# State stages on four whole PSUM banks shared by both diagonals, without filler stages

## The chip, the cores and the metric

The kernel runs on one core of one Trainium2 chip. Five engines have instruction queues of their own, each worked off in order: TensorE (PE in the profile, its weight loads PEld), VectorE (DVE), ScalarE (ACT), GpSimd (POOL) and SyncE (SP), which issues the DMAs here. Matmul results go to PSUM, whose 128 partitions have eight banks of 512 float32 each; DVE and ACT read them there. The metric is the device time of one execution in microseconds, lower is better, as the median of several runs.

## The reference

First a delta rule over 768 steps, for each of 4 batches and 8 heads, with a state of 48 x 48; then a gated MLP over the heads' joined outputs.

```python
for t in range(S):                       # S = 768, per batch and head
    kt, vt, bt = k_n[:, :, t], v[:, :, t], beta[:, :, t, None]
    y[:, :, t] = einsum('bhd,bhde->bhe', q[:, :, t], state)
    v_old = einsum('bhde,bhd->bhe', state, kt)
    state = state + bt[..., None] * einsum('bhd,bhe->bhde', kt, vt - v_old)
x = y.transpose(0, 2, 1, 3).reshape(B, S, H * D)
h = maximum(x @ w_in, 0);  u, v = halves of h
v_n = (v - mean(v)) / sqrt(var(v) + 1e-6)
v_s = einsum('ts,bsd->btd', w_spatial, v_n) + b_spatial[None, :, None]
out = (u * v_s) @ w_out
```

k_n is k divided by its norm. All inputs are float32, and the output has shape 4 x 768 x 384.

## The kernel before

The recurrence is worked in chunks of 64 steps: 12 chunks for each of 4 batches, 48 chunk steps s. Two chains run beside each other: batches 0 and 2 in one, 1 and 3 in the other, six chunks behind; ORDER interleaves them. A chunk step handles all 8 heads, as 4 units of two heads each; one head of a unit lies on partitions 0 to 63, the other on 64 to 127.

Each chunk step has stages on PE of 8 small matmuls (64 x 64 blocks, two heads by four units; step d has 16). A stage writes a tile `pt` in PSUM, and one instruction on DVE or ACT reads it, the stage's reader:

- kk (L574): k times k, ahead of time; reader DVE L595, which makes the matrix to be inverted in `ta`
- e and f (L705): complete the inverse T of that matrix; readers ACT L717 (`pi`) and ACT L729 (`ta`)
- a (L733): state times k; reader DVE L748 (`vk`)
- b (L753): T times that; reader DVE L764 (`us`)
- c (L773): update of the state; reader DVE L792 (`st`)
- qk (L796): q times k; reader DVE L808 (`aq`)
- d (L814): the chunk's output; reader ACT L837 (`xs`)

The chain through the state is a, b, c and again a of the same chain's next chunk. T comes from DVE: groups of four chunk steps are bounced through DRAM, inverted lane by lane with products and sums (`lanes`, L635 and L642) and bounced back.

A 64 x 64 stage uses half of PE's 128 x 128 array: its two heads lie either on the diagonal (kind "diag": e, f, c, qk) or on the other one (kind "anti": kk, a, b, d). One stage of each kind can run together, their matmuls issued in turn.

The MLP (L894 to L1069) has matmuls over the whole array ("full"): v and u from the finished outputs of four chunks, g with w_spatial when a whole batch is there, and o with w_out. They use the banks `pm` and, once the last lanes are done, `pw`.

The order in which each engine gets its instructions is not written by hand. A planner (class Line) runs when the program is built: every job is a generator that yields its next Op with an engine, an estimated occupancy and latency, a function that says when its inputs are ready, and a due time. Line.step takes the engine that can begin first and, among the operations ready within a small slack, the one with the earliest due time. For PE, Line.tensor chooses between full operations and stages. It takes a full operation when the activity of the last 3.4 us (area) is low and one is ready; otherwise an urgent operation, a pair of kinds, a full one, or a single stage. keep_warm inserts matmuls on `ones` (L1239) when PE would be idle and activity is low. Once a stage is picked, L179 looks for one of the other kind that is ready within 0.2 us. If there is none and the area is below FILL, a filler (L1248) takes its place: as many matmuls on `mpos`, into a free tile of the other kind, whose result nobody reads.

The result of every stage goes to a slot of a Slots object: take gives the slot that came free first, and the job gives it back when the planner has placed the reader. Before, four banks `pt0` to `pt3` are cut into eight halves of 256 columns. Each kind has four slots, two halves each of two banks:

```python
banks = [ps.tile([128, 512], F32, name=f"pt{i}") for i in range(4)]
halves = [x[:, o : o + 256] for x in banks for o in (0, 256)]
...
slots = {"anti": Slots(halves[:4]), "diag": Slots(halves[4:])}
```

tiles_op (L414) makes a stage's Op: it is ready when its inputs are and a slot of its kind is free. The planner knows slots only by these free times. The waits on semaphores that the chip executes are derived by the framework from the tiles that the instructions touch.

Of the kernel before, what the change touches and what calls it, by code (L numbers as in the profile page):

```python
# [72 lines left out]
class Line:  # L73
# [4 lines left out]
    def __init__(self, t0):  # L78
        self.t = dict.fromkeys(("PE", "DVE", "ACT", "POOL", "SP"), t0)
        self.done = {}  # L80
        self.jobs = []
        self.mode = "full"
        self.cur = 0
        self.hist = []
        self.idle = self.fake = None

    def at(self, *names):
        done = self.done
# [64 lines left out]
    def tensor(self, e0, near):  # L153
        tiles = [f for f in near if f[1].kind != "full"]
        full = [f for f in near if f[1].kind == "full"]

        def first(fs):
            return min(fs, key=lambda f: (f[1].due(), f[0]), default=None)

        kinds = {k: [f for f in tiles if f[1].kind == k] for k in ("anti", "diag")}  # L160
        low = self.area(e0) < LOW
        urgent = [f for f in near if f[1].due() <= self.cur + URGENT]
        pick = first(full) if low else first(urgent)
        if pick is None and all(kinds.values()):
            if self.mode == "tile" or not full or first(tiles)[1].due() <= self.cur + PAIR:
                pick = first(tiles)
        pick = pick or first(full) or first(tiles)
        t, op, j = pick
        self.keep_warm(t)
        t = max(t, self.t["PE"])  # L170
        change = 0.12 if (op.kind == "full") != (self.mode == "full") else 0.0
        slow = self.slow(t)
        if op.kind == "full":
            self.mode = "full"
            self.t["PE"] = t + change + op.occ * slow
            self.hist.append((self.t["PE"], op.occ * 2300))
            return self.grant(j, t + change + op.occ * slow + op.lat - op.occ)
        self.mode = "tile"
        f = first([f for f in kinds["anti" if op.kind == "diag" else "diag"] if f[0] <= t + 0.2])  # L179
        picked = [(op, j)]  # L180
        if f:
            picked.append(f[1:])
            t = max(t, f[0])
        lists = [o.make() for o, _ in picked]
        act_ = sum(o.lat * len(x) for (o, _), x in zip(picked, lists))
        if not f and self.area(t) < FILL:
            more = self.fake("anti" if op.kind == "diag" else "diag", t, len(lists[0]))
            if more:
                lists.append(more)
                act_ += 62 * len(more)  # L190
        for k in range(max(map(len, lists))):
            for x in lists:
                if k < len(x):
                    x[k]()
        end = t + change + 0.056 * slow * max(map(len, lists))
        self.t["PE"] = end
        self.hist.append((end, act_))
        for _, k in picked:
            self.grant(k, end + 0.22)
# [36 lines left out]
def delta_rule_gated_mlp(  # L236
# [107 lines left out]
    sss, nrs, t0s = ([sb(f"{n}{i}", G * NU) for i in range(2)] for n in ("ss", "nr", "t0"))  # L344

    banks = [ps.tile([128, 512], F32, name=f"pt{i}") for i in range(4)]
    halves = [x[:, o : o + 256] for x in banks for o in (0, 256)]
    pms = [ps.tile([128, 512], F32, name=f"pm{i}") for i in range(2)]
    pws = [ps.tile([128, 512], F32, name=f"pw{i}") for i in range(2)]

    class Slots:
        def __init__(self, tiles):
            self.free = [(0.0, k, x) for k, x in enumerate(tiles)]

        def ready(self):
            return min(self.free)[0] if self.free else None

        def take(self):
            f = min(self.free)
# [3 lines left out]
        def give(self, x, t):  # L363
            self.free.append((t, *x))

    slots = {"anti": Slots(halves[:4]), "diag": Slots(halves[4:])}
    ob_s = Slots([sb(f"ob{i}", DM) for i in range(1)])
    tmp_s, pm_s, xs_s, vh_s, ub_s = Slots(tmps), Slots(pms), Slots(xsb), Slots(list(zip(vhs, vls))), Slots(ubs)

# [27 lines left out]
    def rows_s(h):  # L397
        return rows_t(1 - h)
# [9 lines left out]
    def psl(t, w):  # L408
        return t[:, : NU * w].rearrange("p (u e) -> p u e", e=w)

    def mm(*a, **k):
        return lambda: nc.tensor.matmul(*a, **dict(dict(start=True, stop=True), **k))  # L412

    def tiles_op(kind, dep, d, build, w):  # L414

        held = []

        def make():
            x = slots[kind].take()
            held.append(x)  # L420
            return build(psl(x[1], w))

        return Op("PE", 0, 1.3 * w, both(dep, slots[kind].ready), d, kind, make), held


    def load_w(buf, hi, lo, src, d):
# [147 lines left out]
    def kk(t):  # L574
        g = t // G
        d = due(4 * g - 9)
        k = kts[t % 2] if t >= 2 * G else (
            xsb[t // 4][0:KR, t % 4 * 256 : t % 4 * 256 + 256].rearrange("p (u t) -> p u t", t=CH)
        )
        yield dma(at(("pk", t - 2) if t >= 2 * G + 2 else None), due(4 * g - 11), 3.5 if t < 2 * G else 6.0, 1.0)  # L580
        nc.sync.dma_start(out=k, in_=kq_t[t][:, 0])
        landed = line.t["SP"] + (3.0 if t < 2 * G else 5.5)
        free = [("b", s) for s in range((g - TG) * G, (g - TG) * G + G)] if g >= TG else []
        op, held = tiles_op(
            "anti",
            both(on(landed), at(("mc", t) if t >= G else None, *free)),
            d,
            lambda p: [mm(p[rows_t(h), u], k[rows_d(h), u, :], k[rows_d(h), u, :]) for u, h in UH],
            CH,
        )  # L590
        x = yield op
        done["pk", t] = x
        x = yield dve(both(on(x), at(("mc", t))), d, 256)
        p = held[0]
        nc.vector.tensor_tensor(out=t_of(t), in0=psl(p[1], CH), in1=mcs[t % 2], op=ALU.mult)  # L595
        slots["anti"].give(p, x)
        done["kk", t] = x

    ad_g = {}
# [105 lines left out]
    def step_ef(s):  # L705
        tt, tn, pi = t_of(s), tns[s % 2], pis[s % 2]
        op, held = tiles_op(
            "diag",
            at(("t", s), ("f", s - 2) if s >= 2 else None),
            due(s - 1),  # L710
            lambda p: [mm(p[rows_t(h), u], tt[rows_t(h), u, :], tn[rows_t(h), u, :]) for u, h in UH],
            32,
        )
        x = yield op
        done["e", s] = x
        x = yield act(on(x), due(s - 0.9), 128, 1)
        nc.scalar.mul(out=pi[:, :, 0:32], in_=psl(held[0][1], 32), mul=hl)  # L717
        slots["diag"].give(held[0], x)
        op, held = tiles_op(
            "diag",  # L720
            on(x),
            due(s - 0.8),
            lambda p: [mm(p[rows_t(h), u], pi[rows_t(h), u, :], tt[rows_t(h), u, 32:64]) for u, h in UH],
            32,
        )
        x = yield op
        done["f", s] = x
        x = yield act(on(x), due(s - 0.7), 128)
        nc.scalar.copy(out=tt[:, :, 32:64], in_=psl(held[0][1], 32))  # L729
        slots["diag"].give(held[0], x)  # L730
        done["fa", s] = x

    def step_ab(s):  # L733
# [3 lines left out]
        if c:  # L737
            op, held = tiles_op(
                "anti",
                at(("S", s), ("kq", s), ("vs", s)),  # L740
                due(s - 0.5),
                lambda p: [mm(p[rows_t(h), u], kq[rows_d(h), 0, u, :], cols(st, u, rows_d(h))) for u, h in UH],
                HD,
            )
            x = yield op
            done["a", s] = x
            x = yield dve(on(x), due(s - 0.45), 192)
            nc.vector.tensor_add(out=v, in0=v, in1=psl(held[0][1], HD))  # L748
            slots["anti"].give(held[0], x)
        else:  # L750
            done["a", s] = x = 0.0
        old = prev(s, 2)
# [14 lines left out]
            in1=css[s // G][:, s % G].unsqueeze(2).broadcast_to([128, NU, HD]),  # L767
            op=ALU.mult,
        )
        slots["anti"].give(held[0], x)  # L770
        done["U", s] = x

    def step_c(s):  # L773
# [16 lines left out]
        x = yield dve(on(x), due(s + 0.12), 192)  # L790
        lo = slice(0, KR)
        nc.vector.tensor_add(out=heads(nx, lo), in0=heads(st, lo), in1=psl(held[0][1], HD)[lo])  # L792
        slots["diag"].give(held[0], x)
        done["S", PLACE[b, c + 1]] = x

    def step_qk(s):  # L796
# [9 lines left out]
        done["qk", s] = x  # L806
        x = yield dve(on(x), due(s + 0.85), 256)
        nc.vector.tensor_tensor(out=aq, in0=psl(held[0][1], CH), in1=mall, op=ALU.mult)  # L808
        slots["diag"].give(held[0], x)
        done["q", s] = x  # L810

    xcur = {}
# [1 line left out]
    def step_d(s):  # L814
# [20 lines left out]
        xt = xcur[ch][1].rearrange("p (u t) -> p u t", t=256)  # L835
        x = yield act(on(x), due(s + 1.3), 256)
        nc.scalar.mul(out=xt[0:112, :, qt * 64 : qt * 64 + 64], in_=psl(held[0][1], CH)[0:112], mul=-1.0)  # L837
        slots["anti"].give(held[0], x)
        done["xs", s] = x
        if qt == 3:  # L840
            line.spawn(convert((b * NC_ + c) // 4, xcur[ch], x))
# [392 lines left out]


    def idle(t):
        free = [f[2][:, 0:256] for k in (pm_s, slots["anti"], slots["diag"]) for f in k.free if f[0] <= t]
        if free:
            nc.tensor.matmul(  # L1239
                free[0].rearrange("p (n t) -> p n t", t=128),  # L1240
# [4 lines left out]
            )  # L1245
        return bool(free)

    def fake(kind, t, n):  # L1248

        free = [f[2] for f in slots[kind].free if f[0] <= t]  # L1250
        if not free:
            return None
        p = psl(free[0], HD)
        r = [
            mm(p[rows_t(h) if kind == "diag" else rows_s(h), u], mpos[rows_t(h)], mpos[rows_t(h), 0:HD])
            for u, h in UH
        ]
        return (r * 2)[:n]

    line.idle, line.fake = idle, fake  # L1260
    ET = mybir.EngineType
    with tc.manual_schedule(engines={ET.PE, ET.DVE, ET.Activation, ET.Pool, ET.SP}):
        seen = {"s": 0, "g": 0}
# [74 lines left out]
```

## Time and profile before

| | |
|---|---|
| median of 3 runs | 595.15 us (591.41, 595.15, 597.2) |
| the profiled execution | 594.68 us, span of its instructions 593.0 us |
| mean granted TensorE clock in it | 0.902 |
| matmuls on ones (L1239) | 228 |
| filler matmuls (mpos, L412) | 288 |
| DMA moved | 64.31 MB, mean 108 GB/s |

The profile is of one execution. A group's row has the line of the kernel, the engine, the operation, output<-inputs by the program's names without their numbers, the shape and the count; then the busy time in us, the mean of one in ns, and the time that the engine was idle before such instructions, with what released it. A timeline's row has start and duration in us, engine, line, operation, and in brackets the idle time before it and the releaser. All stages are recorded at L412, the helper that issues their matmuls; the operands tell them apart.

The span has three parts. Up to some 60 us the first chunks' inverse is made and weights are loaded. From 60 to 400 us the chains and the lanes run with MLP work between them, and behind 400 us the MLP's work prevails, with the last stages in between until 530 us.

### The profile page before, as it was taken

The page shows a single profiled execution, that of the slowest core. Times are in us where ns is not written, and L with a number is a line of the kernel's source. Part 1 is how long each engine was busy: PE and PEld are TensorE (multiplying, and loading weights), DVE is VectorE, ACT ScalarE, POOL GpSimd, SP SyncE. Part 2 cuts the span into 40 slices and gives each one's busy share as a digit, 9 for nine tenths or more (in the row PEclk, how much of TensorE's full clock was granted, in tenths as well). Part 3 has the DMA queues.
Part 4 walks back from the last instruction along what each step waited for, and adds up shares of the span by engine and source line. Part 5 has one row for each costly group of instructions (what it writes and reads, how often), then busy time and mean ns, then how long its engine had stood idle before and what let it go on. Part 6 is the DMA issues. An engine that isn't in the chain of part 4 may idle for free.

```text
span 593.0 us, 22265 instructions
## 1 busy us (share of the span) xinstructions
PE 521.4 (88%) x9404; PEld 474.3 (80%) x9404; DVE 352.9 (60%) x1436; ACT 216.8 (37%) x536; POOL 139.5 (24%) x210
## 2 busy tenths in 40 slices
PE   5935889889778997979999989999999999988997
PEld 5834868778657786979997878889988899977996
DVE  5799585977857988857995685871135422132220
ACT  3224334532334556223326456321256511155111
POOL 5452233652235242312204153120000000000000
PEclk9675586978878999979999899999999999997999
DMA  8767385676935766457736536333012200010001
GB/s 222 213 109 168 92 175 146 182 193 135 222 99 132 178 138 134 103 148 143 179 67 118 154 86 141 120 92 77 28 32 72 67 14 15 28 33 2 1 28 55
DMA packets 140160, 64.31 MB, mean 108 GB/s; under 512 B 107542, under 2 KB 130204, under 8 KB 140060
## 3 DMA queue, kind: packets, MB, share of 16 engines
q1 hardware_dynamic: 140060, 62.88, 43.7%
q8 instruction: 74, 1.21, 0.9%
q14 instruction: 26, 0.21, 0.1%
HBM read 47.55 MB, written 14.02 MB: 104 GB/s over the span
## 4 chain that ended last, share of the span: by engine, by line
PE 58%; DVE 18%; DMA 8%; SPq 6%; issue 5%; ACT 4%; POOL 1%; DVEq 0%; ACTq 0%; POOLq 0%
PE pt L412 21%; PE pm L1001 9%; PE pm L969 6%; PE pw L1001 6%; DVE prod L635 4%; DVE pw L642 4%; PE pm L1056 4%; PE pm L903 3%; PE pw L1056 3%; PE pw L903 2%; DMA kq<-in_kq_t 2%; PE pw L969 1%; SPq L861 1%; DVE ta L595 1%; SPq L619 1%
## 5 line engine op out<-in xcount | busy, mean ns | idle before, releaser
L642 DVE TENSOR_TENSOR pw<-pw,prod 128x30 f32<-128x30 f32 (+6 forms) x330 | 81.6, 251 | 5.4
L635 DVE TENSOR_TENSOR prod<-pw,la 128x30 f32<-128x30 f32 (+6 forms) x330 | 78.7, 241 | 6.9 <-ACT pw L629 1.7
L412 PE MATMUL pt<-kq,st 48*64 48x64 f32 x768 | 56.3, 239 | 2.1 <-ACT xs L837 1.7
L1001 PE MATMUL pm<-wsp_h,vh 128*128 128x256 f32 x192 | 57.4, 299 | 0.0
L412 PE MATMUL pt<-aq,us 64*64 64x64 f32 x768 | 54.4, 235 | 3.3 <-issue 3.0
L1001 PE MATMUL pm<-wsp_l,vh 128*128 128x256 f32 x192 | 54.7, 285 | 0.0
L1001 PE MATMUL pm<-wsp_h,vl 128*128 128x256 f32 x192 | 54.6, 284 | 0.0
L688 POOL TENSOR_TENSOR vk<-vk,cn 128x192 f32<-128x192 f32 x48 | 24.5, 512 | 116.7 <-DMA vk<-in_vk_nat 97.9
L412 PEld LDWEIGHTS pt<-aq,us 64*64 64x64 f32 x768 | 45.0, 149 | 3.5 <-issue 3.1
L412 PEld LDWEIGHTS pt<-kq,st 48*64 48x64 f32 x768 | 44.8, 148 | 3.6 <-ACT xs L837 1.8
L569 POOL TENSOR_TENSOR mc<-mpos,cn 128x256 f32<-128x256 f32 x46 | 28.9, 638 | 62.1 <-DVE cn L557 27.9
L412 PE MATMUL pt<-kq 48*64 48x64 f32 x768 | 37.9, 241 | 5.3 <-DMA kq<-in_kq_t 3.9
L412 PE MATMUL pt<-tn,ta 64*64 64x32 f32 x768 | 35.3, 237 | 7.3 <-DVE tn L703 3.8
L1239 PE MATMUL pm<-ones 128*128 128x256 f32 x216 | 39.5, 333 | 2.5 <-ACT ones L274 2.5
L1037 ACT CAST gh<-tmp 128x512 fp32r<-128x512 f32 x24 | 14.8, 619 | 70.3 <-DVE tmp L1018 70.2
L412 PE MATMUL pt<-us,vk 64*64 64x48 f32 x704 | 33.6, 235 | 7.5 <-DVE us L764 6.6
L412 PEld LDWEIGHTS pt<-tn,ta 64*64 64x64 f32 x768 | 30.8, 154 | 10.9 <-DVE tn L703 5.7
L412 PE MATMUL pt<-ta,pi 64*64 64x32 f32 x768 | 35.5, 235 | 3.8 <-ACT pi L717 2.0
L412 PE MATMUL pt<-k 48*64 48x64 f32 x640 | 30.4, 242 | 9.2 <-DMA k<-in_kq_t 6.8
L1001 PEld LDWEIGHTS pm<-wsp_h,vh 128*128 128x128 f32 x192 | 36.9, 192 | 1.5
L1018 DVE TENSOR_TENSOR tmp<-pm,ub 128x512 f32<-128x512 f32 x16 | 11.0, 688 | 45.4 <-PE pm L1004 45.4
L412 PEld LDWEIGHTS pt<-us,vk 64*64 64x64 f32 x704 | 28.1, 147 | 12.0 <-DVE us L764 8.8
(182 smaller groups left out, 1500.4 us busy)
## 6 DMA issues: line engine op xcount, KB each, us to landing
kq<-in_kq_t SPq DMA_DIRECT2D x48, 224.0 KB, 3.5
vk<-in_vk_nat SPq DMA_DIRECT2D x48, 200.0 KB, 3.4
ad<-ta SPq DMA_DIRECT2D x24, 256.0 KB, 4.2
la<-ad SPq DMA_DIRECT2D x44, 128.0 KB, 4.0
out<-ob SPq DMA_DIRECT2D x24, 192.0 KB, 1.9
k<-in_kq_t SPq DMA_DIRECT2D x40, 112.0 KB, 3.5
knn<-in_k_nat SPq DMA_DIRECT2D x10, 384.0 KB, 4.4
wd<-w SPq DMA_DIRECT2D x22, 128.0 KB, 3.6
```

Source lines behind the costliest of these rows:

```text
L412: return lambda: nc.tensor.matmul(*a, **dict(dict(start=True, stop=True), **k))
L569: (nc.vector if t in (0, 2) else nc.gpsimd).tensor_tensor(out=mc, in0=mall, in1=cns[t // G][:, t % G, 1].unsqueeze(2).broadcast_to([128, N ...
L635: nc.vector.tensor_tensor(out=pr, in0=w[:, :n, j : j + 1].broadcast_to([128, n, m]), in1=la[:, j, j + 1 : 32].unsqueeze(1).broadcast_to([1 ...
L642: nc.vector.tensor_add(out=w[:, :n, j + 1 : 32], in0=w[:, :n, j + 1 : 32], in1=pr)
L688: nc.gpsimd.tensor_tensor(out=v, in0=v, in1=cns[s // G][:, s % G, 0].unsqueeze(2).broadcast_to([128, NU, HD]), op=ALU.mult)
L903: nc.tensor.matmul(p[1], a[:, kt, ts], w[:, kt, DH:], start=(n == 0), stop=(n == 3 * NK - 1))
L969: nc.tensor.matmul(pu[:, k], w[:, kt, d0 : d0 + 128], a[:, kt], start=(n == 0), stop=(n == 3 * NK - 1))
L1001: nc.tensor.matmul(pg[:, k], v[:, d0 : d0 + 128], w[:, si, ts], start=(n == 0), stop=False)
L1018: nc.vector.tensor_tensor(out=gt, in0=pg, in1=ut[:, hs], op=ALU.mult)
L1037: nc.scalar.copy(out=gh[:, hs], in_=gt)
L1056: nc.tensor.matmul(p[1][:, :DM], a[:, dd, ts], w[:, dd], start=(n == 0), stop=(n == 3 * ND - 1))
L1239: nc.tensor.matmul(free[0].rearrange("p (n t) -> p n t", t=128), ones, ones.unsqueeze(1).broadcast_to([128, 2, 128]), start=True, stop=True,)
```

## The change

The eight halves become four slots, the first 256 columns of each of the four banks, in one Slots object for both kinds. A stage of either kind takes whichever came free first. A second stage is only paired with the picked one if two slots are free by then (`room`, the time at which the second slot is free, at most 0.2 us after the first stage's time), and the pair starts no earlier than that. The fillers go. All `slots["anti"]` and `slots["diag"]` in the steps become `st_s`; the matmuls, readers, due times and costs stay.

```diff
-        f = first([f for f in kinds["anti" if op.kind == "diag" else "diag"] if f[0] <= t + 0.2])
+        room = self.room(2)
+        other = kinds["anti" if op.kind == "diag" else "diag"]
+        f = None
+        if room is not None and room <= t + 0.2:
+            f = first([f for f in other if f[0] <= t + 0.2])
         picked = [(op, j)]
         if f:
             picked.append(f[1:])
-            t = max(t, f[0])
+            t = max(t, f[0], room)
         lists = [o.make() for o, _ in picked]
         act_ = sum(o.lat * len(x) for (o, _), x in zip(picked, lists))
-        if not f and self.area(t) < FILL:
-            more = self.fake("anti" if op.kind == "diag" else "diag", t, len(lists[0]))
-            if more:
-                lists.append(more)
-                act_ += 62 * len(more)
...
     banks = [ps.tile([128, 512], F32, name=f"pt{i}") for i in range(4)]
-    halves = [x[:, o : o + 256] for x in banks for o in (0, 256)]
...
-        def ready(self):
-            return min(self.free)[0] if self.free else None
+        def ready(self, n=1):
+            return sorted(self.free)[n - 1][0] if len(self.free) >= n else None
...
-    slots = {"anti": Slots(halves[:4]), "diag": Slots(halves[4:])}
+    st_s = Slots([x[:, 0:256] for x in banks])
+    line.room = st_s.ready
...
         def make():
-            x = slots[kind].take()
+            x = st_s.take()
             held.append(x)
             return build(psl(x[1], w))
 
-        return Op("PE", 0, 1.3 * w, both(dep, slots[kind].ready), d, kind, make), held
+        return Op("PE", 0, 1.3 * w, both(dep, st_s.ready), d, kind, make), held
...
-        free = [f[2][:, 0:256] for k in (pm_s, slots["anti"], slots["diag"]) for f in k.free if f[0] <= t]
+        free = [f[2][:, 0:256] for k in (pm_s, st_s) for f in k.free if f[0] <= t]
...
-    def fake(kind, t, n):
-
-        free = [f[2] for f in slots[kind].free if f[0] <= t]
-        if not free:
-            return None
-        p = psl(free[0], HD)
-        r = [
-            mm(p[rows_t(h) if kind == "diag" else rows_s(h), u], mpos[rows_t(h)], mpos[rows_t(h), 0:HD])
-            for u, h in UH
-        ]
-        return (r * 2)[:n]
-
-    line.idle, line.fake = idle, fake
+    line.idle = idle
```

More of the change, by code (lines that the diff above doesn't have):

```diff
@@ L84, in __init__ @@
         self.hist = []
-        self.idle = self.fake = None
+        self.idle = self.room = None
     def at(self, *names):
@@ L595, in kk @@
         nc.vector.tensor_tensor(out=t_of(t), in0=psl(p[1], CH), in1=mcs[t % 2], op=ALU.mult)
-        slots["anti"].give(p, x)
+        st_s.give(p, x)
         done["kk", t] = x
@@ L717, in step_ef @@
         nc.scalar.mul(out=pi[:, :, 0:32], in_=psl(held[0][1], 32), mul=hl)
-        slots["diag"].give(held[0], x)
+        st_s.give(held[0], x)
         op, held = tiles_op(
@@ L729, in step_ef @@
         nc.scalar.copy(out=tt[:, :, 32:64], in_=psl(held[0][1], 32))
-        slots["diag"].give(held[0], x)
+        st_s.give(held[0], x)
         done["fa", s] = x
@@ L748, in step_ab @@
             nc.vector.tensor_add(out=v, in0=v, in1=psl(held[0][1], HD))
-            slots["anti"].give(held[0], x)
+            st_s.give(held[0], x)
         else:
@@ L769, in step_ab @@
         )
-        slots["anti"].give(held[0], x)
+        st_s.give(held[0], x)
         done["U", s] = x
@@ L792, in step_c @@
         nc.vector.tensor_add(out=heads(nx, lo), in0=heads(st, lo), in1=psl(held[0][1], HD)[lo])
-        slots["diag"].give(held[0], x)
+        st_s.give(held[0], x)
         done["S", PLACE[b, c + 1]] = x
@@ L808, in step_qk @@
         nc.vector.tensor_tensor(out=aq, in0=psl(held[0][1], CH), in1=mall, op=ALU.mult)
-        slots["diag"].give(held[0], x)
+        st_s.give(held[0], x)
         done["q", s] = x
@@ L837, in step_d @@
         nc.scalar.mul(out=xt[0:112, :, qt * 64 : qt * 64 + 64], in_=psl(held[0][1], CH)[0:112], mul=-1.0)
-        slots["anti"].give(held[0], x)
+        st_s.give(held[0], x)
         done["xs", s] = x
```

## The prediction

> **What bounds the kernel now.** I read the page first: its engine shares and the chain that ended last.
>
> ```profile
> span 593.0 us, 22265 instructions
> PE 521.4 (88%) x9404; PEld 474.3 (80%) x9404; DVE 352.9 (60%) x1436; ACT 216.8 (37%) x536; POOL 139.5 (24%) x210
> PE 58%; DVE 18%; DMA 8%; SPq 6%; issue 5%; ACT 4%; POOL 1%; DVEq 0%; ACTq 0%; POOLq 0%
> PE pt L412 21%; PE pm L1001 9%; PE pm L969 6%; PE pw L1001 6%; DVE prod L635 4%; DVE pw L642 4%; PE pm L1056 4%; PE pm L903 3%; PE pw L1056 3%; PE pw L903 2%; DMA kq<-in_kq_t 2%; PE pw L969 1%; SPq L861 1%; DVE ta L595 1%; SPq L619 1%
> ```
>
> PE bounds it, and the largest line of the chain is L412, the stages that the change touches. Next, the busy time by stretch: the recurrence's part and the part behind it have different limits. The columns are length, then PE, PEld, DVE, ACT and POOL busy, granted clock, DMA share, GB/s.
>
> ```profile
> 60.00:150.00 90.00, 78.16 (x1810) 70.25 (x1800) 66.16 (x301) 35.17 (x91) 36.79 (x45) 0.77 0.63 154
> 150.00:260.00 110.00, 91.56 (x2141) 78.92 (x2136) 85.84 (x395) 47.08 (x126) 36.29 (x49) 0.91 0.63 148
> 260.00:400.00 140.00, 134.55 (x2802) 121.50 (x2802) 101.06 (x427) 55.96 (x139) 38.25 (x47) 0.96 0.52 119
> 400.00:530.00 130.00, 127.01 (x1542) 118.82 (x1542) 37.40 (x103) 44.26 (x103) 2.03 (x4) 1.00 0.14 41
> ```
>
> Some of that PE time is the keep-warm matmul on ones (L1239), no work. The same stretches for that line alone (PE, PEld, clock):
>
> ```profile
> 60.00:150.00 90.00, 13.54 (x66) 10.25 (x66) 0.77 0.63 154
> 150.00:260.00 110.00, 4.30 (x28) 3.59 (x28) 0.91 0.63 148
> 260.00:400.00 140.00, 2.43 (x16) 2.03 (x16) 0.96 0.52 119
> ```
>
> From 60 to 400 us PE was idle for 11.8 + 18.4 + 5.5 = 35.7 us and on ones for 20.3 us: 56 us is all that shorter waits of the stages could give there. Behind 400 us PE is full of the MLP's work, idle for 3 us of 130: whatever PE gains or loses before goes into the end one for one.
>
> Now the stages, by the view that keeps shapes apart: PE busy, mean ns of one, then PE's idle time before them and who ended it. Sixteen records are a stage, thirty-two for step d, whose second half (aq,us) shares its time.
>
> ```profile
> L412 PE MATMUL pt<-kq,st 48*64 48x64 f32 x768 | 56.3, 239 | 2.1 <-ACT xs L837 1.7 <-DVE ta L595 0.3
> L412 PE MATMUL pt<-kq 48*64 48x64 f32 x768 | 37.9, 241 | 5.3 <-DMA kq<-in_kq_t 3.9 <-ACT pi L717 1.3
> L412 PE MATMUL pt<-vk,ta 64*64 64x48 f32 x768 | 35.6, 234 | 2.4 <-ACT ta L729 1.1 <-DVE vk L748 0.8 <-issue 0.2
> L412 PE MATMUL pt<-ta,pi 64*64 64x32 f32 x768 | 35.5, 235 | 3.8 <-ACT pi L717 2.0 <-ACT xs L837 0.7 <-issue 0.7
> L412 PE MATMUL pt<-tn,ta 64*64 64x32 f32 x768 | 35.3, 237 | 7.3 <-DVE tn L703 3.8 <-DMA ta<-wd 2.9 <-ACT pi L717 0.5
> L412 PE MATMUL pt<-us,vk 64*64 64x48 f32 x704 | 33.6, 235 | 7.5 <-DVE us L764 6.6 <-DVE prod L635 0.6
> L412 PE MATMUL pt<-st,kq 48*64 48x48 f32 x704 | 32.0, 233 | 5.0 <-DMA kq<-in_kq_t 3.3 <-DVE st L792 0.7 <-ACT xs L837 0.5
> L412 PE MATMUL pt<-k 48*64 48x64 f32 x640 | 30.4, 242 | 9.2 <-DMA k<-in_kq_t 6.8 <-DVE ta L595 1.6 <-ACT xs L837 0.5
> L412 PE MATMUL pt<-xs 48*64 48x64 f32 x128 | 6.0, 267 | 0.2 <-DVE ta L595 0.2
> ```
>
> They add to 302.6 us for 376 stages. The union of all of L412, fillers included, is much shorter:
>
> ```profile
> sum 593.00, PE 197.20 PEld 175.67; mean PE 16.43 PEld 14.64
> ```
>
> Pairs (one stage of each diagonal, interleaved) and overlapping neighbours thus save at least 105 us. Followed through the timeline, the 376 stages run as 126 pairs and 124 lone bursts.
>
> Odd in the rows above are releasers that no operand explains. Step qk reads kq alone, yet waited 1.3 us for ACT's read at L717; kk reads k alone, yet waited for L595 and L837. What is left is the output's bank: before, two halves of one bank go to stages of one kind in turn. The plainest place in the timeline:
>
> ```profile
> 171.78 0.67 PE L412 MATMUL pt<-vk,ta 64*64 64x48 f32 x16
> 172.83 0.37 PE L412 MATMUL pt<-kq,st 48*64 48x64 f32 x1
> 174.38 0.43 PE L412 MATMUL pt<-aq,us 64*64 64x64 f32 x4
> 174.85 0.36 DVE L764 TENSOR_TENSOR us<-pt,cs 128x192 f32<-128x192 f32 x1 [3.18 <-PE pt L412]
> ```
>
> Step b (vk,ta) was done at 172.45, but its reader began at 174.85, 0.04 us after the next stage of the same diagonal, a step d with which it shares nothing but the bank. It cost DVE 2.4 us, and the step c behind it as much. The other way round, a stage that waits for the other half's reader:
>
> ```profile
> 118.38 0.36 ACT L837 ACTIVATE xs<-pt 112x256 f32<-112x256 f32 x1
> 118.80 0.37 PE L412 MATMUL pt<-kq,st 48*64 48x64 f32 x1 [1.68 <-ACT xs L837]
> ```
>
> This is the first step d of the second chain (s = 7), which by L829 needs no xs; it waited 1.68 us for that of the first.
>
> **The change part by part.** The planner lists all five queues anew, so every row's place may move; no instruction but the fillers goes, no DMA is added, and SP's and POOL's queues are moved only as their steps' times shift.
>
> Fillers. Their rows, first 100 us and sum (PE alone):
>
> ```profile
> 0.00:100.00 100.00, 11.03 (x208) 0.68 0.67 161
> sum 593.00, PE 13.98; mean PE 3.50
> ```
>
> 288 matmuls, 18 groups, 13 of them in the first 100 us. They lie interleaved with a lone stage, which takes as long with a partner as without:
>
> ```profile
> 204.57 0.25 PE L412 MATMUL pt<-vk,ta 64*64 64x48 f32 x1
> 204.58 0.24 PE L412 MATMUL pt<-tn,ta 64*64 64x32 f32 x1
> 205.07 0.67 PE L412 MATMUL pt<-kq 48*64 48x64 f32 x16
> ```
>
> The pair holds PE for 205.07 - 204.57 = 0.50 us, the lone stage lasts 0.67. So the cover is the stage itself, and taking them out gives 0; between -14 us (all of it was on the path) and +8 (the clock falls, rival 3). I take 0, for the cover is seen.
>
> Whole banks, first half: PE no longer waits for the reader of another half. Unexplained by operands are 1.7 + 1.3 + 0.7 + 0.5 + 0.5 + 1.6 + 0.5 + 0.2 = 7.0 us in the rows above. Some is a half's own reuse, which stays: between 0 and -7, I take -5. Next late are the operands, mostly the same readers' results.
>
> Whole banks, second half: a reader no longer waits for a later stage of its bank. Followed stage by stage (first-free order gives successive stages of one diagonal the two halves of a bank), 25 DVE readers started within 0.3 us of such a stage's end. The first and last that cost over 0.1 us:
>
> ```profile
> 65.53 0.35 DVE L792 TENSOR_TENSOR st<-st,pt 112x192 f32<-112x192 f32 x1 [2.30 <-PE pt L412]
> 460.27 0.36 DVE L792 TENSOR_TENSOR st<-st,pt 112x192 f32<-112x192 f32 x1 [0.69 <-PE pt L412]
> ```
>
> What DVE idled for that, cut to the time between the own stage's end and the other's, adds to 11.4 us over the 25. DVE is 72 to 78% busy up to 400 us and in order, with the two chains and the lanes' products behind each other, so most counts: between 0 and -11, I take -8. On ACT the same wait is hidden:
>
> ```profile
> ACT pi L717 <- PE pt L412: 42.5, 25, 4.2
> ACT ta L729 <- PE pt L412: 40.0, 25, 5.3
> ```
>
> ACT waits 82 us there without being late for anything but steps f and b, before which PE mostly has MLP work; 0.
>
> One pool of four, and a pair only where two banks are free. A stage holds its bank from its first matmul to its reader's end. In the timeline 19 of 126 pairs began with three or more others unread 0.2 us later; a matmul of the first and of the last:
>
> ```profile
> 64.01 0.31 PE L412 MATMUL pt<-ta,pi 64*64 64x32 f32 x1
> 453.60 0.23 PE L412 MATMUL pt<-kq 48*64 48x64 f32 x1
> ```
>
> Each one split is a burst more: 0.50 us by the spacing above, 0.75 by the mean stage (37.9 / 48 = 0.79, 35.3 / 48 = 0.74). Between 0 (the second finds another partner, or runs in PE's idle time) and 19 x 0.75 = +14; I take half of 19 x 0.50, +5, because many of the nineteen were crowded only by the held readers above. By the Trainium skill, "TensorEngine Tiling (Array Packing)", Gotcha 1: PSUM Pressure, row tiles cannot use one bank at the same time and need different ones, so a pair always costs two of the four; if that split all nineteen at the higher price, the sum below would end 9 us higher. The trace agrees in so far as the two kinds lie in different banks here; no run here shows them in one.
>
> Lone stages: 4 of 124 began with four others unread. A wait there holds back on PE the MLP matmuls queued behind, and then their readers on ACT and DVE: 4 x 0.5 = 2 us at most, nothing at least; I take +1.
>
> Sum: 0 - 5 - 8 + 5 + 1 = -7 us. The profiled execution took 594.68 us (span 593.0 and 1.7 around it), 0.5 below the median of the three, 595.15; so 587.7 against its own time, and 588 against the median.
>
> **The rivals.** (1) Slower: the four banks starve the pairs. All four are busy after two pairs until the first reader is done, and DVE's readers queue behind lanes' products; the planner never waits for a second bank, it sends the stage alone. For it speaks that the pairs save 105 us; against it that 107 of the 126 pairs find room as they stand. At 0.50 us a burst, 26 bursts more eat the gain of 13; with 45 the time is 595 - 13 + 22.5 + 1 = 606 us. It decides from about 36 bursts more (595 - 13 + 18 + 1 = 601, +1%).
>
> (2) No change: the waits go, but the time does not. PE is filled with MLP work during many of them, and the next thing late is a DMA (kq 3.9 + 3.3 us, k 6.8 us in the rows) or T from the lanes. Then only about half of the 13 us returns, and the 6 of the losses eats it: 595 us. That the bank is not what holds the unexplained waits would end here too, or at 595 + 6 = 601.
>
> (3) The clock: fewer matmuls in the thin early part. The stretch from 60 to 150 us had 0.77 of the clock; at 0.74 its 78.16 us would take 81.3 (+3), at 0.70 86 (+8): 591 to 596 with the rest of the sum. Against it: behind 100 us only five fillers ran, and the planner puts ones-matmuls where activity is missing. By the Trainium skill, "TensorE: Matmul & The Clock Gate", Part 1, the array runs at half rate unless the last window of some 3.4 us was busy, and so fillers are worth their place; the trace agrees that the thin stretches have the low clock.
>
> **How the numbers follow.** About 1%, 6 us, is what a measurement of this kernel can tell from no change: faster is below 589.2, slower above 601.1. Forecast 0.50, own range 577 to 592; of it 0.43 lies below 589.2 and 0.07 above. Rival 2 0.25 (same). Rival 1 0.17 (slower). Rival 3 0.08 (half faster or same: 0.02 faster, 0.05 same, 0.01 slower). That makes faster 0.45, same 0.37, slower 0.18. The low end takes all of the bank waits and no loss, 595 - 7 - 11 = 577, less 3 us for half-clock stretches that go with PE's gaps; the high end is rival 1 short of its worst. Range 574 to 604.
>
> **What would show it.** Right: no reader of pt on DVE that starts 0.04 us after an unrelated stage; the wait of L764 for PE well below its 30 us; ones-matmuls and PE idle between 60 and 400 us down by about 10 us; pairs between 105 and 126, and L412's union up by 5 to 10 us less the 0 for the fillers. Wrong: L412's union up by 15 us or more (rival 1); bank waits gone with PE's idle time as before, now ended by DMA or tn (rival 2); granted clock of 60 to 150 us below 0.74 (rival 3). And the planner's new order may move MLP work so that the end has a gap, which none of these steps prices.

## The result and the profile after

The changed kernel takes 568.4 us (median of four, 566.4 to 574.5) against 596.2 us on the same chip: 0.956 of the time before, with a 95% interval of 0.945 to 0.966. The forecast was 588 us with a range of 574 to 604. The direction was right, the size was not: some 27 us went, not 7. Medians here and below are of all executions; the ratios leave out those in a slower state that some executions show.

The page of the changed kernel, lines as before (L411 is the former L412):

```profile
span 567.2 us, 21693 instructions
PE 505.5 (89%) x9095; PEld 463.2 (82%) x9095; DVE 355.6 (63%) x1436; ACT 219.5 (39%) x536; POOL 140.0 (25%) x210
PE 60%; DVE 18%; DMA 10%; issue 4%; ACT 4%; SPq 3%; DVEq 0%; ACTq 0%
PE pt L411 21%; PE pm L1000 9%; PE pw L1000 8%; PE pm L968 6%; PE pm L902 6%; PE pm L1055 4%; DVE pw L641 4%; DVE prod L634 4%; DMA kq<-in_kq_t 2%; PE pw L968 2%; PE pw L1055 2%; DMA ad<-ta 2%; DMA xs<-xs 2%; DMA la<-ad 1%; DVE t L542 1%
```

PE still bounds it, and the chain has the same shape. PE is busy for 505.5 us in place of 521.4, though nothing was taken out but the 288 fillers and 21 of the 228 matmuls on ones. The same stretches (length; PE, PEld, DVE, ACT and POOL busy; granted clock, DMA share, GB/s):

```profile
60.00:150.00 90.00, 73.97 (x1856) 65.54 (x1855) 71.33 (x313) 37.30 (x97) 36.55 (x44) 0.83 0.69 171
150.00:260.00 110.00, 99.93 (x2290) 88.02 (x2289) 93.90 (x440) 51.52 (x130) 39.44 (x54) 0.94 0.65 151
260.00:400.00 140.00, 134.34 (x2562) 124.91 (x2561) 92.99 (x371) 53.66 (x130) 33.30 (x39) 0.99 0.48 111
400.00:530.00 130.00, 129.20 (x1524) 120.24 (x1523) 41.88 (x122) 51.49 (x118) 2.41 (x4) 1.00 0.12 36
530.00:567.00 37.00, 33.27 (x243) 32.62 (x241) 6.92 (x10) 5.98 (x11) 0.00 (x0) 1.00 0.09 32
```

From 60 to 260 us DVE does 165 us of work where it did 152, and the clock is higher in the three stretches up to 400 us (0.83, 0.94, 0.99 for 0.77, 0.91, 0.96). The union of the stages, by the same view for L411:

```profile
sum 567.00, PE 188.90 PEld 170.96; mean PE 31.48 PEld 28.49
```

It fell by 8.3 us, though there are now 119 pairs and 138 lone bursts, 7 bursts more. By the count explained further down, taken of the stages alone, 7.5 of the 8.3 us are matmuls that no longer ran at the half rate. The rows of single stages show where bank waits went; columns as before:

```profile
L411 PE MATMUL pt<-kq,st 48*64 48x64 f32 x768 | 53.2, 229 | 0.6 <-issue 0.5
L411 PE MATMUL pt<-aq,us 64*64 64x64 f32 x768 | 50.9, 224 | 0.8 <-issue 0.5 <-DVE us L763 0.3
L411 PE MATMUL pt<-kq 48*64 48x64 f32 x768 | 36.8, 234 | 7.1 <-DMA kq<-in_kq_t 5.8 <-issue 1.4
L411 PE MATMUL pt<-tn,ta 64*64 64x32 f32 x768 | 35.7, 236 | 11.5 <-DVE tn L702 8.5 <-DVE st L791 1.7 <-DVE pw L641 1.2
L411 PE MATMUL pt<-ta,pi 64*64 64x32 f32 x768 | 35.5, 235 | 2.1 <-ACT pi L716 1.9 <-issue 0.2
L411 PE MATMUL pt<-vk,ta 64*64 64x48 f32 x768 | 35.0, 233 | 1.9 <-DVE vk L747 0.8 <-issue 0.6 <-ACT wout_h L460 0.5
L411 PE MATMUL pt<-us,vk 64*64 64x48 f32 x704 | 32.4, 231 | 1.5 <-DVE us L763 0.8 <-issue 0.6
L411 PE MATMUL pt<-st,kq 48*64 48x48 f32 x704 | 32.0, 230 | 6.7 <-DMA kq<-in_kq_t 2.9 <-DVE st L791 1.8 <-issue 1.6
L411 PE MATMUL pt<-k 48*64 48x64 f32 x640 | 29.9, 240 | 10.5 <-DMA k<-in_kq_t 9.5 <-issue 0.6 <-DVE pw L641 0.4
L411 PE MATMUL pt<-xs 48*64 48x64 f32 x128 | 6.0, 267 | 0.0
```

Step qk, which reads kq alone, now waits for the DMA of kq and no longer for ACT's read at L717; kk waits for its own DMA. Step c (us,vk) had 7.5 us of idle time before it and has 1.5. One reader of a bank is left that no operand explains: step e's 1.7 us for L791, the reader of a c that held the shared bank. In sum, though, PE's idle time before the stages fell only from 46.1 us (with 3.3 before aq,us) to 42.7, for e, qk and kk now wait longer, mostly for their operands. The gain is not in these rows.

Where the 26 us of span are can be counted from the matmul records and the trace's clock, which is either full or half. Take PE's time without the ones-matmuls, and half of what lies in half-rate stretches as lost to the rate:

| profiled execution | span | matmuls at full rate | lost to half rate | rest: idle and ones |
|---|---|---|---|---|
| before | 593.0 | 443.5 | 40.9 | 108.5 |
| after | 567.2 | 442.4 | 27.4 | 97.4 |
| difference | -25.8 | -1.1 | -13.5 | -11.1 |

The work is the same. In this pair of executions half of the gain is idle time, and half is matmuls that ran at the full clock. The pair flatters the clock: the profiled execution of the kernel before had 0.902, where the executions behind the ratios average 0.911, and the changed kernel's had 0.922, with 0.919 on average. Scaled to the averages the loss falls by some 9 us, a third of the gain (an estimate: on average some 106 and 92 us of the span are at the half rate, and the profiles lost 40.9 of 116.4 and 27.4 of 88.7 us). That tells where the time is, not what caused it; for that there are the experiments.

### The profile page after: what moved, and what is told of

It reads as the page before. It is cut to its first block, busy times and chain, and to the rows that moved or that the text cites. A ratio compares the mean times of both kernels' runs of the same rounds, so it can differ in the third digit from the quotient of the medians.

```text
span 567.2 us, 21693 instructions
## 1 busy us (share of the span) xinstructions
PE 505.5 (89%) x9095; PEld 463.2 (82%) x9095; DVE 355.6 (63%) x1436; ACT 219.5 (39%) x536; POOL 140.0 (25%) x210
## 4 chain that ended last, share of the span: by engine, by line
PE 60%; DVE 18%; DMA 10%; issue 4%; ACT 4%; SPq 3%; DVEq 0%; ACTq 0%
PE pt L411 21%; PE pm L1000 9%; PE pw L1000 8%; PE pm L968 6%; PE pm L902 6%; PE pm L1055 4%; DVE pw L641 4%; DVE prod L634 4%; DMA kq<-in_kq_t 2%; PE pw L968 2%; PE pw L1055 2%; DMA ad<-ta 2%; DMA xs<-xs 2%; DMA la<-ad 1%; DVE t L542 1%
## 5 line engine op out<-in xcount | busy, mean ns | idle before, releaser
L641 DVE TENSOR_TENSOR pw<-pw,prod 128x96 f32<-128x96 f32 (+10 forms) x330 | 81.3, 250 | 4.9
L634 DVE TENSOR_TENSOR prod<-pw,la 128x126 f32<-128x126 f32 (+12 forms) x330 | 78.8, 242 | 6.4 <-ACT pw L628 1.4
L411 PE MATMUL pt<-kq,st 48*64 48x64 f32 x768 | 53.2, 229 | 0.6 <-issue 0.5
L411 PE MATMUL pt<-aq,us 64*64 64x64 f32 x768 | 50.9, 224 | 0.8 <-issue 0.5
L1000 PE MATMUL pm<-wsp_h,vh 128*128 128x256 f32 x168 | 49.3, 294 | 0.2 <-ACT vh L944 0.2
L1000 PE MATMUL pm<-wsp_h,vl 128*128 128x256 f32 x168 | 47.7, 284 | 0.2 <-DVE vl L948 0.2
L1000 PE MATMUL pm<-wsp_l,vh 128*128 128x256 f32 x168 | 47.7, 284 | 0.0
L411 PE MATMUL pt<-tn,ta 64*64 64x32 f32 x768 | 35.7, 236 | 11.5 <-DVE tn L702 8.5
L411 PEld LDWEIGHTS pt<-kq,st 48*64 48x64 f32 x768 | 42.6, 139 | 2.0 <-issue 1.3
L411 PEld LDWEIGHTS pt<-tn,ta 64*64 64x64 f32 x768 | 31.6, 153 | 14.4 <-ACT knn L533 5.4
L411 PE MATMUL pt<-kq 48*64 48x64 f32 x768 | 36.8, 234 | 7.1 <-DMA kq<-in_kq_t 5.8
L411 PEld LDWEIGHTS pt<-aq,us 64*64 64x64 f32 x768 | 42.3, 139 | 0.5 <-DVE us L763 0.5
L1238 PE MATMUL pm<-ones 128*128 128x256 f32 x201 | 40.1, 343 | 2.5 <-ACT ones L273 2.5
L411 PE MATMUL pt<-k 48*64 48x64 f32 x640 | 29.9, 240 | 10.5 <-DMA k<-in_kq_t 9.5
L411 PE MATMUL pt<-st,kq 48*64 48x48 f32 x704 | 32.0, 230 | 6.7 <-DMA kq<-in_kq_t 2.9
L411 PE MATMUL pt<-ta,pi 64*64 64x32 f32 x768 | 35.5, 235 | 2.1 <-ACT pi L716 1.9
L411 PEld LDWEIGHTS pt<-kq 48*64 48x64 f32 x768 | 29.8, 143 | 8.8 <-issue 4.2
L411 PE MATMUL pt<-vk,ta 64*64 64x48 f32 x768 | 35.0, 233 | 1.9 <-DVE vk L747 0.8
L1238 PEld LDWEIGHTS pm<-ones 128*128 128x128 f32 x201 | 32.4, 232 | 4.7 <-ACT ones L273 2.5
```

What stands on the lines that cost most here:

```text
L634: nc.vector.tensor_tensor(out=pr, in0=w[:, :n, j : j + 1].broadcast_to([128, n, m]), in1=la[:, j, j + 1 : 32].unsqueeze(1).broadcast_to([1 ...
L641: nc.vector.tensor_add(out=w[:, :n, j + 1 : 32], in0=w[:, :n, j + 1 : 32], in1=pr)
L1000: nc.tensor.matmul(pg[:, k], v[:, d0 : d0 + 128], w[:, si, ts], start=(n == 0), stop=False)
L1238: nc.tensor.matmul(free[0].rearrange("p (n t) -> p n t", t=128), ones, ones.unsqueeze(1).broadcast_to([128, 2, 128]), start=True, stop=True,)
```

## The experiments

Three things were changed at once: the bank that holds a result, the slots with which the planner reckons (and so the order of everything), and the fillers. Theory W: the waits through the bank that two halves share. Rival O: the new order. Ratios are to the kernel before, with a 95% interval. Where a run is said to keep an order, every engine has the same instructions in the same sequence as in the kernel named, and only the place of the results differs.

**The changed kernel's order on half banks.** The planner runs with four slots, but each result lies in the first free of four halves of its kind, as before. Every engine has the changed kernel's instructions in the same order.

```diff
...
+    place = {"anti": Slots(halves[:4]), "diag": Slots(halves[4:])}
...
-            x = st_s.take()
-            held.append(x)
+            n = st_s.take()
+            x = place[kind].take()
+            held.append((n[0], x[1], kind, x, n))
             return build(psl(x[1], w))
```

> The changed kernel's planner and every engine's order are kept, but a stage's result lies where the kernel before put it: in the first free of four half banks of its kind. Theory W (waits through the bank that two halves share are what the change removed): most of the gain goes, 583 to 597 us, and readers of pt on DVE start 0.04 us after an unrelated stage again. Rival O (the gain is the new order of the planner, with the pool and the pair rule): the time stays with the changed kernel, 565 to 575 us.

Measured: 578.0 us (574.0 to 580.2), 0.967 (0.960 to 0.975). That is between the two expectations: 10 us of the gain go with the half banks, and 17 us remain with the order and the absence of fillers. In the order of the instructions 66 of the 376 stages start beside an unread half here, 60 in the kernel before and none in the changed one; 39 readers here, 40 before and none in the changed kernel wait for the semaphore of a later stage in the other half. One place of this run, step b of a chunk; the timeline of PE and DVE:

```profile
252.64 0.25 PE L416 MATMUL pt<-vk,ta 64*64 64x48 f32 x2
253.81 0.23 PE L416 MATMUL pt<-aq,us 64*64 64x64 f32 x2
254.07 0.36 DVE L769 TENSOR_TENSOR us<-pt,cs 128x192 f32<-128x192 f32 x1 [0.73 <-PE pt L416]
```

and the same instructions in the changed kernel:

```profile
250.62 0.22 PE L411 MATMUL pt<-vk,ta 64*64 64x48 f32 x1
250.78 0.17 DVE L641 TENSOR_TENSOR pw<-pw,prod 128x30 f32<-128x30 f32 x1
250.89 0.36 DVE L763 TENSOR_TENSOR us<-pt,cs 128x192 f32<-128x192 f32 x1
```

On whole banks the reader follows its stage by 0.05 us and its predecessor on DVE without a gap. On half banks it waits until the next step d, in the other half, is done: 1.2 us behind its own stage, the last 0.73 us of them with DVE idle. The semaphore that it waits for in the program is the one that this d's last matmul raises. The Trainium skill, "PSUM — Partial Sum Buffer", section "PSUM bank collisions raise a hardware error", says that accesses have to be kept apart by bank and quadrant and not by address. The trace agrees in that the two halves are kept apart here, 1.2 us against 0.05; the wait is the program's, and no run lets two engines into the two halves of a bank at once.

**The order before, with the halves in another sequence.** The halves of each kind are listed so that neighbours lie in different banks; the order of all engines stays.

```diff
-    halves = [x[:, o : o + 256] for x in banks for o in (0, 256)]
+    halves = [x[:, o : o + 256] for p in (banks[:2], banks[2:]) for o in (0, 256) for x in p]
```

> The kernel before with its order on every engine; only the four halves of a kind are listed bank by bank in turn, so that two successive stages of a kind lie in different banks and meet again in one bank at every second stage. Theory W: a good part of the bank waits goes without any change of order, 573 to 588 us. Rival O: the order is the old one, so 590 to 600 us.

Measured: 591.5 us (587.1 to 597.4), 0.990 (0.982 to 0.998). It tells little, since the edit did not part the stages: in the order of the instructions, 60 of 376 start in a bank whose other half is unread, as in the kernel before. The next run has the half chosen at each stage, in a bank without an unread result where there is one:

```diff
...
+        f = min(free, key=lambda f: (f[1] ^ 1 not in open_, max(f[0], dict((i, t) for t, i in free).get(f[1] ^ 1, 0.0)), f[1]))
...
-            x = slots[kind].take()
-            held.append(x)
-            return build(psl(x[1], w))
+            n = slots[kind].take()
+            i = lie(kind)
+            held.append((n[0], halves[i], kind, i, n))
+            return build(psl(halves[i], w))
```

> The kernel before with its order on every engine; only the half bank that a stage gets is chosen so that its bank's other half holds no unread result where that is possible. In the order of the instructions 21 of 376 stages then start beside an unread half, where the kernel before has 60 and the run with alternating halves had 60 as well. Theory W (the bank waits are worth some 10 us at any order): 580 to 588 us. Rival O (at the old order the waits are covered): 590 to 600 us.

Measured: 587.6 us (585.3 to 590.1), 0.992 (0.988 to 0.995). With a third of the shared starts left, 5 us (by the ratio) to 6 us (by the medians) went at the old order: W, at its weak end.

**Without fillers.** The kernel before, with `if False:` for the filler's condition.

> The kernel before without filler stages (288 matmuls that nobody reads); halves, kinds and slots as before. Theories W and O: fillers lie beside lone stages, 589 to 601 us. Rival F (the fillers took PE time or held readers up): 585 us or less, with L412's union shorter by 8 us or more. Rival C (fillers keep the clock up): over 601 us with a lower granted clock up to 150 us.

Measured: 587.7 us (586.0 to 593.7), 0.988 (0.980 to 0.995). This was 8 us less, between the ranges, and L412's union was 3.4 us shorter (193.8 for 197.2 us), where rival F asked for 8. But leaving out fillers also changes what the planner takes for PE's activity, and so the order. Whether it was the fillers or the order was tested with two more orders, below.

**Two whole banks for each kind.** Slots as `halves[0:4:2]` and `halves[4:8:2]`; fillers stay.

> The kernel before with two whole banks for each kind in place of four halves; fillers stay, no sharing between kinds. Theory W: no bank holds two stages, so most of the gain is there though the planner has two slots a kind, 568 to 585 us. Rival P (sharing all four banks between the kinds is what helps, and two slots a kind starve PE): 588 us or more.

Measured: 573.3 us (564.6 to 575.5), 0.954 (0.942 to 0.966). In this order whole banks give the gain without sharing and with fillers.

**How much an order is worth.** One constant of the planner, the slack within which PE's operations compete (0.25 us), gives other orders with the same rules:

```diff
-    SLACK = {"PE": 0.25, "DVE": 0.03, "ACT": 0.05, "POOL": 0.05, "SP": 0.05}
+    SLACK = {"PE": 0.22, "DVE": 0.03, "ACT": 0.05, "POOL": 0.05, "SP": 0.05}
```

> The kernel before with one planner constant moved (the slack within which PE's operations compete, 0.25 to 0.22 us): another order, same slots, same fillers. Theory L (of the 27 us, some 10 are the whole banks and the rest is that one order of the planner is luckier than another): the time moves by several us, 576 to 594. Rival S (fillers and the four shared slots give better orders as such): 590 to 602 us, as before.

> As the run before it, with a slack of 0.28 us. Theory L: 576 to 600 us, and not the time of the run with 0.22. Rival S: 590 to 602 us.

> The changed kernel with the slack at 0.22 us. Theory L: another draw, 565 to 588 us, on average some 10 us below the same two draws of the kernel before. Rival S: 563 to 573 us, as the changed kernel.

> The changed kernel with the slack at 0.28 us. Theory L: 562 to 588 us. Rival S: 563 to 573 us.

The last two orders were then also laid on half banks, and the kernel before was run at both without fillers:

> The order of the changed kernel with slack 0.22 us (579 us on whole banks), laid on half banks by kind as in the first run of this kind. Theory W: 585 to 593 us. Rival (the difference of 10 us at the slack of 0.25 was of that order alone): 575 to 583 us.

> The order of the changed kernel with slack 0.28 us (568 us on whole banks), laid on half banks by kind. Theory W: 574 to 584 us. Rival: 564 to 572 us.

> The kernel before with slack 0.22 us and no filler stages. If the fillers cost time as such (they were worth 6 to 8 us at the slack of 0.25): 580 to 585 us against 590 with them. If that was the luck of one order: 585 to 596 us.

> The kernel before with slack 0.28 us and no filler stages. If the fillers cost time as such: 578 to 583 us against 588 with them. If not: 584 to 596 us.

All of them, as medians in us and ratios:

| slack | 0.22 | 0.25 | 0.28 | mean ratio |
|---|---|---|---|---|
| before | 589.9 (0.988) | 1.000 | 588.4 (0.988) | 0.992 |
| before, no fillers | 593.8 (0.998) | 587.7 (0.988) | 587.8 (0.988) | 0.991 |
| after's planner, half banks | 593.8 (1.002) | 578.0 (0.967) | 582.6 (0.986) | 0.985 |
| after (whole banks) | 579.1 (0.975) | 568.4 (0.956) | 568.4 (0.958) | 0.963 |

Down the last two rows only the place of the results differs, and each order loses time on halves: 14.7, 9.6 and 14.2 us by the medians, 2.2 points of the ratio on average, 13 us. At 0.25 alone the two intervals still touch (0.945 to 0.966 and 0.960 to 0.975); at the other two they don't (0.970 to 0.981 and 0.998 to 1.005; 0.951 to 0.965 and 0.978 to 0.993). Over three orders no worth of the fillers can be seen (0.992 and 0.991 on average; without them 4 us more, 8 less and 1 less), so the 8 us of the first try were its order. Along a row the same rules spread by 1 to 3.5%, that is 6 to 21 us: the order that a planner happens to find. Against the forecasts: 593.8 us on half banks ended 1 us above theory W's range, and the kernel before took nearly the same time with 0.28 as with 0.22, which theory L had not expected; the others lie in the ranges of L, of W, or of fillers that cost nothing as such, and 568.4 us with 0.28 lies in rival S's range too.

**Sharing, without fillers.** Two whole banks a kind, no fillers, no rule for pairs:

> Two whole banks for each kind, no fillers, no sharing and no rule for pairs. If the shared pool is worth something: 574 to 585 us, over the changed kernel's 568. If only whole banks count: 562 to 575 us.

Measured: 579.9 us (577.9 to 583.5), 0.978 (0.973 to 0.984). By itself this lies in the range of a shared pool that is worth something. But with the fillers, in another order, it was 0.954; the mean, 0.966, is the shared pool's 0.963 within the spread of orders. That sharing brings nothing is not shown, but no gain of it could be seen.

**The clock as a cause of its own.** The changed kernel with FILL = 9000 or 2500 for 4000, the activity up to which planned gaps of PE are filled with matmuls on ones:

> The changed kernel with the activity up to which planned gaps of PE are filled with matmuls on ones raised from 4000 to 9000 (405 matmul records more). Theory K (half of the gain is the granted clock, and stretches at half rate come from PE's gaps): less time at half rate and 558 to 566 us. Rival (the stretches come from gaps that the planner does not see, or the fillers delay work): 567 to 580 us.

> The changed kernel with the activity up to which planned gaps are filled lowered from 4000 to 2500. If matmuls on ones delay work more than their clock brings: 558 to 567 us. If the clock they keep is needed: 570 to 585 us with a granted clock below 0.91.

With more: 596.1 us (590.5 to 599.7), 1.003 (0.998 to 1.008), all of the gain gone and above both ranges. Its clock, and the sum of its L1238 over all stretches:

```profile
core 0: 594.0 us, clock 0.945
```

```profile
sum 594.00, PE 103.40 PEld 84.15; mean PE 17.23 PEld 14.03
```

The clock rose from 0.922 to 0.945, as theory K expected, and the loss to half rate fell from 27.4 to 25.1 us in the count above; but the ones took 103.4 us where the changed kernel has

```profile
sum 567.00, PE 40.98 PEld 33.17; mean PE 6.83 PEld 5.53
```

and PE's idle time fell by only 26.5 us for those 62.4. The rest, it seems, stood in front of work. Part of the 28 us can be the order, which changes here too; but the changed kernel's three orders lie only 11 us apart. With fewer: 572.9 us (565.6 to 573.4), 0.963 (0.956 to 0.970), in the range for a clock that is needed, but neither faster nor slower than the changed kernel beyond the spread; the clock was 0.912 where it was expected below 0.91. Its order is another as well. So a higher clock bought with matmuls on ones was no gain here.

What the clock has to do with the banks shows in the three pairs of one order. Same count as in the table above, half banks to whole banks: lost to half rate 35.3 to 27.4, 34.3 to 29.8 and 39.8 to 31.2 us; rest 100.4 to 97.4, 111.3 to 100.8 and 96.2 to 95.5 us. In each pair 4.5 to 8.5 us are matmuls that no longer ran at half rate. These are single executions, but the mean clock of all of them goes the same way: 0.916 to 0.919, 0.913 to 0.921 and 0.911 to 0.924. That bank waits leave PE thin enough to lose the clock fits this; no run held the clock fixed to show it.

## Why the prediction was right in its main step and wrong in its size

- **The bank waits (-5 and -8, together -13 us): right.** At an unchanged order they measure 9.6, 14.7 and 14.2 us, 13 on average. These are orders of the changed planner; at the order before, 39 of 60 shared starts were worth 5 to 6 us. That the size agrees so well is partly luck, since 5 and 8 were picked within 0 to 7 and 0 to 11. DVE's part shows: its idle time before its readers of pt, as far as a stage on PE ended it, falls from 52.7 to 46.6, 59.6 to 49.8 and 58.3 to 52.1 us in the three pairs, for 8 forecast. How the waits act was only half seen: the forecast counted idle time of PE and DVE, and about half of the difference in the three pairs' profiles came as half-rate matmuls.
- **L764 as a sign: wrong.** Its wait for PE fell as forecast, from 30 us to 7.8 (before, then after):

```profile
L764 DVE TENSOR_TENSOR us<-pt,cs 128x192 f32<-128x192 f32 x48 | 16.9, 353 | 30.5 <-PE pt L412 30.2
L763 DVE TENSOR_TENSOR us<-pt,cs 128x192 f32<-128x192 f32 x48 | 16.9, 353 | 8.2 <-PE pt L411 7.8
```

In the changed order on half banks it is nearly as short:

```profile
L769 DVE TENSOR_TENSOR us<-pt,cs 128x192 f32<-128x192 f32 x48 | 17.0, 354 | 11.1 <-PE pt L416 10.8
```

So most of that fall was order, and the sign would not have told W from O.

- **Fillers at 0: right**, as far as three orders can tell. The reading behind it set the spacing of a pair (0.50 us) against the whole length of a lone stage (0.67); by the same rows the pair's length is 0.68, so it holds. In the profile before, the stages' matmuls cover 197.2 us with the fillers and 197.2 without: none ran by itself.
- **Split pairs (+5) and lone stages (+1): the first about right as a count, not confirmed as a cost.** Seven bursts more at 0.50 us are 3.5 us of PE's time, but no loss is seen: on half banks the changed planner's three orders average 0.985 against 0.992. Within the spread of orders a cost of a few us can't be ruled out. The forecast that L412's union would grow by 5 to 10 us failed; it fell by 8.3. In the changed order on half banks, with the same bursts, it is

```profile
sum 578.00, PE 196.71 PEld 176.71; mean PE 32.79 PEld 29.45
```

so the fall came with the whole banks. By the count above 7.4 of these 7.8 us are half-rate time.
- **"The planner lists all five queues anew", priced at nothing: the step that failed.** The text named the new order as something that none of its steps prices, and then gave it no width. By the means in the table, the 4.45% are: 0.8 from the order before to the mean of its rule, 0.7 from one planner's mean to the other's (within the spread, so not shown), 2.2 for the whole banks, and 0.75 from the mean of the changed kernel's orders to the one it has. Two draws of an order, both in favour, are some 9 us: that is luck, and the forecast had no term for it. With the 6 us of losses that did not show and the 4 us from one planner's mean to the other's they make the difference between -7 and -27. A mean of three orders is itself good to a few us only, so these shares, all but that of the whole banks, are estimates.
- **The range's low end (574):** it took the bank waits at their highest and 3 us for the clock, and no draw of the order. With an estimated 5 us either way for each of the two orders it would have reached below 570.
- **Rivals.** (1), too few banks for pairs, did not happen: 119 pairs of 126. (2), the waits go but not the time, did not happen either. (3), the clock, went the other way: 0.77 to 0.83 between 60 and 150 us.
- **PE idle and ones between 60 and 400 us, down by about 10:** they fell from 56 to 52 us at fixed times, but over the whole span from 108.5 to 97.4, since later work moved into these stretches. The sign should have been set for the whole span.

## What to carry to other kernels

Two halves of a PSUM bank were one resource in these runs: a reader of one half waited for matmuls into the other, and a planner that counts them as two free slots makes an order whose waits it can't see. Fewer slots that are really free were better here than more that are not. Where a change alters a planner's order, run it and the old rule with a constant moved a little, before a few per cent are put down to the change, and lay the new order on the old resources to part the two.

## What the runs showed that was not expected

With half-rate time counted half, the matmuls without ones take 441.5 to 448.9 us in every one of the profiled executions; nearly all of the differences between 563 and 595 us of span are loss to the half rate (25 to 44 us) and idle time with ones (91 to 121 us). And a higher mean clock went with a slower kernel: 0.945 at 594.0 us against 0.922 at 567.2.
